# A recurrent attention and mixing kernel on one core: scores of half-blocks that are always zero left out, and DMAs dealt out to other queues

## The chip, the core and the metric

The kernel runs on one core of a Trainium2 chip. TensorE multiplies matrices, VectorE and ScalarE do elementwise work, GpSimd does a little of it and issues DMAs, and SyncE only issues DMAs. The metric is the device time of one execution in microseconds (us), and less is better. A run of "before" gave 459.9 us in the median of three (458.04 to 461.52).

## The reference

Two stages follow each other. The first is a gated linear recurrence over 768 time steps for 4 batches and 8 heads of 48 channels; the second is a channel-mixing layer with a width of 384 and an inner width of 1024. Everything is float32.

```python
mag = sqrt(a_re**2 + a_im**2); scale = minimum(mag, 0.999) / (mag + 1e-6)
for t in range(768):                         # per batch and head, S is 48x48
    S = (a_re + i*a_im)[t] * scale[t] * S + k[t] (x) v[t]     # complex S, k and v real
    y[t] = q[t] @ real(S)
x  = y with the heads side by side           # (4, 768, 384)
xk = mu_k * x + (1 - mu_k) * x_previous_step ;  xr likewise with mu_r
v  = relu(xk @ w_k)**2 @ w_v
out = sigmoid(xr @ w_r) * v
```

## The kernel before

**Tiling.** The 4 x 768 steps are cut into eight units of 384 steps (`U`); two units make a batch, and the second of the two continues the state of the first. A unit has three chunks of 128 steps (`NC`). For a unit u, `gate(u)` loads the gates, keys and queries (tile `g`) and the values (tile `v`), turns the gates into running logs and phases on ScalarE and VectorE, and multiplies keys and queries by them in place, so that the recurrence becomes a masked attention inside a chunk and a state carried between chunks. `attend(u)` does that attention: `stack(h)` copies one head's scaled real and imaginary parts of keys and queries by small DMAs from `g` into a `kq` buffer of 112 rows (48, a gap of 16 that is zero, 48); `scores(h)` multiplies keys by queries for the three chunks of one head into a PSUM bank (tile `sc`, line 885), and VectorE multiplies the result by a triangular mask of zeros and ones into `pt` (line 889); `advance(c)` transposes the keys (tile `tr`) and adds keys times values (`up`) to the state; `values(p)` computes the output of two heads, one in each half of the array's columns (tile `y`, line 908 from `pt`, line 915 from the state). Small DMAs move the result `ys` into the transposed activations `xt` (line 930). `mix(u)` forms the mixed inputs, and on TensorE the r gate (three products, tile `z`), the first layer (eight products, also `z`) and the second (eight, tile `o`). From the second unit on, each float32 operand is split into two parts of a faster float32 form, so that a product is nine matmuls instead of three.

**Masked half-blocks.** The scores of a chunk are a block of 128 keys by 128 queries. A key later than the query counts for nothing: the mask has zeros there. So the quarter of 64 late keys by 64 early queries is computed and multiplied by zero.

**Order of the work.** Nothing is ordered by hand. Every step is handed to a planner (class `Plan`) with its engine, an estimated cost, what it reads and writes and which buffers it uses. The planner works out due times backwards from a position in TensorE's work (the table `AT` gives each unit's attention and mixing a stretch) and then plays the execution through; a free engine takes the ready operation that is due first. The order in which operations started in the play is the order in which they are put into the engines' queues, and an engine goes through its queue strictly in order. In that play SyncE's and GpSimd's DMAs have a time line each (`dma[e]`), as if both could transfer at full rate beside each other.

**Queues.** SyncE's queue issues the first unit's `g` loads, the stack moves (line 816), the `xt` moves (line 930) and the stores (line 537). GpSimd's issues all bulk loads else: `g` of the later units (651), `v` (658), the weights (`raw`, 363) and a second load of the weights for a range test (`again`, 627), whose steps are spread over the whole run. GpSimd also clears the gap rows of the six `kq` buffers at the start (351). While the first mixing is not ready, TensorE gets filler products (`warm`, line 966).

Of the kernel before, what the change touches and what calls it, by code (L numbers as in the profile page):

```python
# [11 lines left out]
F32 = mybir.dt.float32  # L12
# [9 lines left out]
C = H * D  # L22
# [7 lines left out]
NP = H // 2  # L30
HR = 64
YS = 3
# [11 lines left out]
AT = ((0.38, 0.74), (1.0, 1.45), (1.28, 1.33), (2.34, 3.3), (2.2, 2.89), (3.4, 4.43), (3.07, 3.65), (4.24, 5.39),  # L44
      (4.34, 4.39), (4.94, 6.44), (5.25, 5.8), (7.11, 7.17), (6.14, 7.38), (7.41, 9.17), (7.2, 7.7), (9.54, 10.42))
PAIRS = 0, 1, 2, 3
# [5 lines left out]
RB = 4  # L52
SIG = 2.5
PTS = 3
# [4 lines left out]
FILL = ("r0", 0, 0), ("z", 0, 0)  # L59
NATIVE = 1  # L60
# [9 lines left out]
class Plan:  # L70
# [11 lines left out]
    QUEUE = dict(SP=0.63, GP=1.1)  # L82
    START, ARRIVE = 1.15, 0.9
    TURN = {("once", "half"): 0.09, ("full", "half"): 0.09,
# [71 lines left out]
    def run(self):  # L156
# [13 lines left out]
        dma = dict.fromkeys(self.QUEUE, 0.0)  # L170
        work = {}
        free, held, got = {}, dict.fromkeys(self.bufs, 0), dict.fromkeys(self.bufs, 0)
        taken, waiting, events, ends, order = set(), {}, [self.BEGIN], [], []
# [7 lines left out]
        def can(i):  # L181

            if ready[i] > t or (ops[i]["table"] and ops[i]["table"] != tables[-1]):
                return False
# [9 lines left out]
        while len(order) < len(ops):  # L194
# [7 lines left out]
            while found:  # L202
                found = False
                for e, queue in list(waiting.items()):
# [29 lines left out]
                    if e in self.QUEUE:  # L234
                        free[e] = t + self.QUEUE[e]
                        dma[e] = max(dma[e], t + self.START) + cost
                        end = dma[e] + self.ARRIVE
# [33 lines left out]
def tile_kernel(ctx, tc, gat, vt, w_all, mu, slow_g, slow_v, out):  # L271
# [51 lines left out]
    def op_dma(n, f, **kw):  # L323

        plan[0].op("SP", n / 360, f, **kw)

    def op_dma_gp(n, f, **kw):

        plan[0].op("GP", n / 300, f, **kw)
# [5 lines left out]
    mask = keep.tile([P, P], F32, name="mask")  # L335
    nc.gpsimd.memset(mask, 1.0)
    nc.gpsimd.affine_select(out=mask, in_=mask, pattern=[[1, P]], compare_op=ALU.is_ge,
                            fill=0.0, base=0, channel_multiplier=-1)
# [11 lines left out]
    for t in kqs:  # L350
        nc.gpsimd.memset(t[32:HR], 0.0)
# [17 lines left out]
    def open_mix(stack):  # L369
# [3 lines left out]

    bufs = dict(ps=5, o=1, xr=1, xk=1, zr=1, x=3, r=RB, hhi=HB, hlo=HB,
                look=1, g=GP, v=5, sq=1, m=1, ph=1, kq=KQ, kt=2, pt=PTS, xt=1, ys=YS)

# [3 lines left out]
    def sigmoid(u):  # L380
        op_act(NT * U, lambda: act(zr[u], zr[u], AF.Sigmoid), table=(u + SIG, "sigmoid"), reads=[("zr", u, mt) for mt in range(NT)],
               writes=[("r", u)], uses=[zr_slot[u]])

    def mix(u, native=False):
# [3 lines left out]
        part_slot = [slot("xr")] * 2 if native else [slot("xk"), slot("xr")]  # L388
        zr_slot[u] = slot("zr")

        def begin(ct):
# [7 lines left out]
            for which in (1, 0):  # L399
                if native:  # L400
                    def whole(which=which):
                        if not hi:
                            x = mp["x"].tile([P, NT, 2, U], F32, tag="xr", name="x")
                            hi.update({0: x[:, :, 0], 1: x[:, :, 1]})
# [48 lines left out]
        def gate_r(mt):  # L453
            sp = slot("ps")
# [5 lines left out]
            def out_():  # L460
                if u not in zr:
                    zr[u] = mp["h"].tile([P, NT, U], F32, tag="zr", name="zr", bufs=1)
                nc.scalar.copy(out=zr[u][:, mt], in_=tiles["z", mt])
            op_pe(cost, mul, kind=kind, reads=parts(1) + [(w_key, W_R + ct) for ct in range(NT)], writes=[("z", u, mt)],
                  uses=[sp, part_slot[1]])
            op_act(U, out_, psum=True, reads=[("z", u, mt)], writes=[("zr", u, mt)], uses=[sp, zr_slot[u]])
        gates_r = [lambda mt=mt: gate_r(mt) for mt in range(NT)]
        if u != NATIVE:
            steps += gates_r
# [56 lines left out]
        if u == NATIVE:  # L526
            steps += gates_r

        def end(mt):
            sr = slot("r")  # L530

# [4 lines left out]
            def store():  # L536
                nc.sync.dma_start(out=out[b, mt * P:(mt + 1) * P, half * U:(half + 1) * U], in_=tiles["y", mt])
# [587 lines left out]
```

## Time and profile before

| what | value |
|---|---|
| runs (us) | 459.9, 458.04, 461.52 |
| profiled execution | 460.59 us, its span 458.6 us |
| granted TensorE clock, mean | 0.945 |
| TensorE busy | 399.6 us, 87% of the span |
| ScalarE, VectorE busy | 341.6 us (74%), 329.3 us (72%) |
| GpSimd busy | 52.2 us (11%) |
| DMA | 67.51 MB |

The span runs from the first to the last instruction of the profiled execution. Times in rows are us from the start of the span unless marked ns. PEld is the loading of weights, which overlaps products. A float32 matmul of this kernel leaves two records. A row names the line of the kernel, the engine, the operation, and the tile written and those read.

### The profile page before, as it was taken

The numbers are of one execution on the slowest core, as the hardware profiler recorded it, in microseconds if no ns is written. First come the engines' busy times: TensorE is split into PE (matmuls) and PEld (weight loads), VectorE is DVE, ScalarE is ACT, GpSimd is POOL, SyncE is SP. The second block draws the span as 40 slices with busy tenths as digits, with TensorE's granted clock in tenths as the row PEclk, the third lists the DMA queues.
The fourth block names the chain that finished last, engine by engine and source line by source line (L and its number), as shares of the span: only waits on it lengthen the run. The fifth ranks groups of instructions, "written<-read, shape, count | busy, mean of one in ns | idle before, by whom it ended". The sixth has DMA issues, their size and how long they took to land.

```text
span 458.6 us, 8780 instructions
## 1 busy us (share of the span) xinstructions
PE 399.6 (87%) x3263; PEld 362.6 (79%) x3263; DVE 329.3 (72%) x536; ACT 341.6 (74%) x591; POOL 52.2 (11%) x116
## 2 busy tenths in 40 slices
PE   2005998999977999999999999999899998999994
PEld 2004995567666999999898989999799997899993
DVE  1599868669849988878886888777897866185222
ACT  5689755987768799989978799789879943563530
POOL 8510020000201120030003000011000000100000
PEclk8555999999978999999999999999999999999998
DMA  8996380602885827383647345268541455300001
GB/s 284 411 410 178 95 290 2 134 22 66 262 189 154 286 55 179 121 281 118 148 127 245 120 112 146 66 216 226 134 135 47 118 135 144 112 4 22 32 1 59
DMA packets 25074, 67.51 MB, mean 147 GB/s; under 512 B 5696, under 2 KB 11840, under 8 KB 25024
## 3 DMA queue, kind: packets, MB, share of 16 engines
q1 hardware_dynamic: 17520, 30.69, 25.6%
q0 software_dynamic: 7504, 36.18, 23.3%
q8 instruction: 28, 0.46, 0.4%
q14 instruction: 22, 0.18, 0.1%
HBM read 38.54 MB, written 4.72 MB: 94 GB/s over the span
## 4 chain that ended last, share of the span: by engine, by line
PE 56%; DMA 16%; ACT 10%; DVE 10%; issue 4%; SPq 2%; POOL 2%; DVEq 0%; ACTq 0%; POOLq 0%
PE z L444 18%; PE o L515 13%; PE sc L885 8%; DMA raw<-in_w_all 4%; DMA xt<-ys 4%; PE y L908 3%; PE o L512 3%; PE up L867 3%; DMA again<-in_w_all 3%; PE y L915 3%; PE z L439 3%; DMA kq<-g 3%; PE tr L847 2%; ACT r L295 2%; SPq L816 1%
## 5 line engine op out<-in xcount | busy, mean ns | idle before, releaser
L444 PE MATMUL z<-x,w 128*128 128x384 f32 x693 | 132.1, 340 | 0.0
L444 PEld LDWEIGHTS z<-x,w 128*128 128x128 f32 x693 | 120.6, 188 | 0.7 <-issue 0.7
L515 PE MATMUL o<-hhi,w 128*128 128x384 f32 x336 | 87.7, 342 | 0.0
L885 PE MATMUL sc<-kq 112*128 112x128 f32 x384 | 57.7, 297 | 5.8 <-DMA kq<-g 4.8
L515 PEld LDWEIGHTS o<-hhi,w 128*128 128x128 f32 x336 | 59.9, 188 | 0.6 <-issue 0.5
L885 PEld LDWEIGHTS sc<-kq 112*128 112x128 f32 x384 | 50.6, 204 | 11.0 <-issue 7.6
L515 PE MATMUL o<-hlo,w 128*128 128x384 f32 x168 | 57.1, 340 | 2.3 <-DVE hlo L496 2.2
L847 PE MATMUL tr<-ident,g 128*128 128x128 f32 x120 | 20.3, 298 | 36.2 <-DVE g L784 36.2
L847 PEld LDWEIGHTS tr<-ident,g 128*128 128x128 f32 x120 | 15.9, 153 | 39.3 <-DVE g L784 37.3
L484 ACT ACTIVATE r<-z 128x384 f32<-128x384 f32 x64 | 30.8, 483 | 20.6 <-PE z L444 20.0
L784 DVE TENSOR_TENSOR g<-g,r 128x768 f32<-128x768 f32 x48 | 43.1, 954 | 3.1 <-ACT r L295 2.9
L889 DVE TENSOR_TENSOR pt<-sc,mask 128x384 f32<-128x384 f32 x64 | 34.6, 552 | 5.4 <-PE sc L885 4.7
L515 PEld LDWEIGHTS o<-hlo,w 128*128 128x128 f32 x168 | 31.5, 188 | 3.9 <-DVE hlo L496 3.9
L423 ACT CAST x<-xm 128x384 fp32r<-128x384 f32 x42 | 21.1, 512 | 17.5 <-DVE xm L415 15.1
L488 ACT ACTIVATE h<-r 128x384 f32<-128x384 f32 x64 | 33.0, 520 | 0.8
L496 DVE TENSOR_TENSOR hlo<-h,hhi 128x384 fp32r<-128x384 f32 x56 | 30.9, 554 | 2.4 <-ACT hhi L311 1.0
L295 ACT ACTIVATE sq<-m 128x1152 f32<-128x1152 f32 (+2 forms) x27 | 28.0, 1054 | 6.1 <-DVE m L732 3.7
L908 PE MATMUL y<-pt,v 128*64 128x128 f32 (+1 forms) x384 | 29.3, 280 | 3.0 <-DVE pt L889 3.0
L311 DVE CAST hhi<-h 128x384 fp32r<-128x384 f32 x33 | 11.8, 358 | 25.9 <-PE o L515 13.4
L908 PEld LDWEIGHTS y<-pt,v 128*64 128x64 f32 (+1 forms) x384 | 20.8, 129 | 11.5 <-issue 5.8
L289 ACT ACT_TABLE_LOAD x22 | 28.2, 1283 | 1.2 <-PEq L1114 0.8
L627 POOL DMA_DIRECT2D again<-in_w_all x19 | 10.2, 539 | 161.9 <-ACT again L634 114.4
(85 smaller groups left out, 687.9 us busy)
## 6 DMA issues: line engine op xcount, KB each, us to landing
kq<-g SPq DMA_DIRECT2D x96, 144.0 KB, 3.4
g<-in_gat POOLq DMA_DIRECT2D x18, 768.0 KB, 6.4
again<-in_w_all POOLq DMA_DIRECT2D x19, 384.0 KB, 3.7
raw<-in_w_all POOLq DMA_DIRECT2D x9, 768.0 KB, 10.3
v<-in_vt POOLq DMA_DIRECT2D x24, 192.0 KB, 6.2
out_t<-y SPq DMA_DIRECT2D x24, 192.0 KB, 3.2
xt<-ys SPq DMA_DIRECT2D x48, 72.0 KB, 3.2
kq<-g SPq DMA_DIRECT2D x32, 96.0 KB, 3.1
```

The costliest lines, as they stand in the source:

```text
L289: nc.scalar.add_instruction(mybir.InstLoadActFuncSet(name=nc.get_next_instruction_name(), act_func_set_id=loaded[0], engine=mybir.EngineTy ...
L295: nc.scalar.activation(out=out, in_=in_, func=func, **kw)
L444: nc.tensor.matmul(z, lhsT=wt[s[0]][:, part, s[1]], rhs=r[which][:, ct], start=n == 0, stop=n == 3 * NT - 1)
L484: nc.scalar.activation(out=t["r", j], in_=t["f", j], func=AF.Relu)
L488: nc.scalar.activation(out=t["h", j], in_=t["r", j], func=AF.Square)
L496: nc.vector.tensor_tensor(out=t["lo", j], in0=t["h", j], in1=t["hi", j].bitcast(F32), op=ALU.subtract)
L515: nc.tensor.matmul(tiles["o", mt], lhsT=wt[W_V + 2 * j][:, part, ts(mt, P)], rhs=r, start=j == 0 and n == 0, stop=j == NJ - 1 and n == 2)
L784: nc.vector.tensor_tensor(out=g[:, ct, 2 * i:2 * i + 2], in0=g[:, ct, 2:4], in1=t["r"][:, ct, 1 - i:2 - i].to_broadcast([P, 2, U]), op=ALU ...
L847: nc.tensor.transpose(out=t["tr", c, part][:, ct * P:(ct + 1) * P], in_=G[u][:, ct, 2 * part, c * P:(c + 1) * P], identity=ident)
L885: nc.tensor.matmul(sc[:, c], lhsT=kq[h][:, 0, ts(c, P)], rhs=kq[h][:, 1, ts(c, P)], start=True, stop=True)
L889: nc.vector.tensor_mul(pts[h], t["sc", h], mask.unsqueeze(1).to_broadcast([P, NC, P]))
L908: nc.tensor.matmul(t["y", p][rows, ts(c, P)], lhsT=V[u][c][:, cols], rhs=pts[hs[j]][:, c], start=c == 0, stop=False)
```

## The change

It has these parts.

1. `scores(k, c)` handles two pairs of heads and one chunk instead of one head and three chunks. Each head is done as two products: the 64 early keys by all 128 queries, and the 64 late keys by the 64 late queries; late keys by early queries are left out. The two heads of a pair use opposite halves of the array's columns. The result of a pair lies in three times 64 columns, and one VectorE instruction per operation takes it apart into two heads by an overlapping access pattern and applies the mask, now all-ones or zero integers, by a bitwise AND over 512 columns. For the second head of a pair the rows come out with the two half-blocks of keys exchanged, so `v` carries a second copy of every second head, rolled by 64 rows: its rows grow from 384 to 576 columns.
2. The four pairs run in the order 0, 3, 1, 2; the scores of two pairs are followed by the values of both.
3. Queues: `g` of the units from 2 on, `v` from unit 1 on and the second weight load go to SyncE's queue; stack moves and `xt` moves may go to either queue, as the planner finds one free. The planner now keeps one DMA time line for both queues, starts a bulk DMA only when that line is not too far behind, and has other costs for issuing (GpSimd 0.65 instead of 1.1 us).
4. The r gate's three products come last in every unit's mixing (before: only in one unit), its sigmoid is taken in three pieces of 384 columns instead of one of 1152, and the final product is written in place. The filler ends with the first product of the first layer.
5. The `kq` gaps are cleared by VectorE; the mask is made by eight small selects on GpSimd. Two more `kq` buffers for the first unit lie in the space of the first unit's mixed input (`x0`).
6. Buffers: `r` 6 for 4 (it now also holds the r gate), `pt` 4 for 3 (of 512 columns instead of 384), `v` 4 for 5, `kt` 1 for 2, `ys` 2 for 3. The table `AT` has other numbers.

The core of the diff:

```diff
-PAIRS = 0, 1, 2, 3
+PAIRS = 0, 3, 1, 2
-FILL = ("r0", 0, 0), ("z", 0, 0)
+FILL = ("r0", 0, 0), ("f", 0, 0)
-    QUEUE = dict(SP=0.63, GP=1.1)
+    QUEUE = dict(SP=0.63, GP=0.65)
+    BULK = 0.4
...
+            if o["engine"] in self.QUEUE and o["cost"] > self.BULK and dma > t + self.START:
+                return False
...
+    def op_move(n, f, **kw):
+        plan[0].op("SP", n / 380, lambda e: f(nc.sync if e == "SP" else nc.gpsimd), other={"GP": n / 380}, **kw)
...
-        nc.gpsimd.memset(t[32:HR], 0.0)
+        nc.vector.memset(t[32:HR], 0.0)
...
-        op_act(NT * U, lambda: act(zr[u], zr[u], AF.Sigmoid), ...
+        for mt in range(NT):
+            op_act(U, lambda mt=mt: act(zr[u, mt], zr[u, mt], AF.Sigmoid), ...
...
-                nc.gpsimd.dma_start(out=raw.bitcast(I32), in_=w_all[:, i * C:(i + 1) * C].bitcast(I32))
+                nc.sync.dma_start(out=raw.bitcast(I32), in_=w_all[:, i * C:(i + 1) * C].bitcast(I32))
...
-                    (nc.gpsimd if u else nc.sync).dma_start(out=G[u][:, ct, part], in_=gat[b, half, ct, :, part])
+                    (nc.gpsimd if u == 1 else nc.sync).dma_start(out=G[u][:, ct, part], in_=gat[b, half, ct, :, part])
...
-                    v = ap.tile([P, C], F32, tag="v", name="v", bufs=5)
-                    nc.gpsimd.dma_start(out=v, in_=vt[b, half, c])
+                    v = ap.tile([P, C + C // 2], F32, tag="v", name="v", bufs=VB)
+                    (nc.sync if u else nc.gpsimd).dma_start(out=v, in_=vt[b, half, c])
...
-            def scores(h):
+            def scores(k, c):
...
-                    for c in range(NC):
-                        nc.tensor.matmul(sc[:, c], lhsT=kq[h][:, 0, ts(c, P)], rhs=kq[h][:, 1, ts(c, P)], start=True, stop=True)
+                    for i, p in enumerate(ps2):
+                        for late in range(2):
+                            for j in range(2):
+                                rows = slice((j ^ late) * Q, (j ^ late) * Q + Q)
+                                q = kq[2 * p + j][:, 1, c * P + late * Q:(c + 1) * P].rearrange("p (b t) -> p b t", t=Q)
+                                cols = slice((1 + late) * Q if j else 0, 3 * Q if j else (2 - late) * Q)
+                                nc.tensor.matmul(sc[rows, i, cols], lhsT=kq[2 * p + j][:, 0, c * P + late * Q:][:, :Q],
+                                                 rhs=q if j else q[:, ::-1], start=True, stop=True)
...
-                    nc.vector.tensor_mul(pts[h], t["sc", h], mask.unsqueeze(1).to_broadcast([P, NC, P]))
+                    both = bass.AP(tensor=sc.tensor, offset=sc.offset, ap=[sc.ap[0], sc.ap[1], [Q, 2], [1, P]])
+                    nc.vector.tensor_tensor(out=pts[k, c].bitcast(I32), in0=both,
+                                            in1=masks.unsqueeze(1).to_broadcast([P, 2, 2, P]), op=ALU.bitwise_and)
...
+            steps += stacks(0) + all_scores(0) + stacks(1)[:2] + adv + [begin] + stacks(1)[2:]
+            a, *rest = all_scores(1)
+            steps += [a] + both(0) + rest + both(1)
```

171 lines of the change are left out of this document (93 added, 78 removed).

## The prediction

> **What bounds the kernel now.** I read the page first (busy shares and the chain that ended last), then the busy times by stretches of 20 us, then the chain in order of time, and last the timelines of the stretches where TensorE is not full. The first fence has two lines of the page's busy shares and chain, and rows of the stretches (us of the stretch; then busy time and instructions of PE, PEld, DVE, ACT, POOL; granted clock; DMA share; GB/s).
>
> ```profile
> PE 399.6 (87%) x3263; PEld 362.6 (79%) x3263; DVE 329.3 (72%) x536; ACT 341.6 (74%) x591; POOL 52.2 (11%) x116
> ...
> PE 56%; DMA 16%; ACT 10%; DVE 10%; issue 4%; SPq 2%; POOL 2%; DVEq 0%; ACTq 0%; POOLq 0%
> ```
>
> ```profile
> 0.00:20.00 20.00, 2.93 (x12) 2.64 (x12) 4.68 (x9) 10.61 (x21) 14.48 (x40) 0.72 0.90 338
> 20.00:40.00 20.00, 0.47 (x1) 0.18 (x1) 19.95 (x29) 17.96 (x28) 3.42 (x5) 0.50 0.92 354
> ...
> 60.00:80.00 20.00, 18.55 (x121) 14.51 (x122) 14.11 (x21) 10.87 (x15) 2.21 (x4) 1.00 0.37 132
> ...
> 120.00:140.00 20.00, 16.06 (x186) 13.13 (x184) 12.18 (x21) 13.71 (x22) 1.61 (x3) 0.83 0.85 213
> 140.00:160.00 20.00, 17.65 (x137) 16.09 (x136) 18.22 (x31) 15.10 (x27) 3.73 (x7) 0.91 0.76 230
> ...
> sum 460.00, PE 399.60 PEld 362.59 DVE 329.29 ACT 341.62 POOL 52.16; mean PE 17.37 PEld 15.76 DVE 14.32 ACT 14.85 POOL 2.27
> ```
>
> The 87% hides three stages. For 40 us TensorE has nothing to do (2.93 + 0.47 us busy, nearly all of it warming). From there to the end it is nearly full: 399.6 - 3.4 = 396.2 us busy. Between 120 and 160 us it idles for 6.3 (40 - 16.06 - 17.65), and the granted clock fell to 0.83 and 0.91 there. So time comes off in two ways: less TensorE work in the full stage, or an earlier start of it. The chain in order of time (start, duration, what) shows who sets the start and the hole after 120 us; the timeline rows (start, duration, instruction, in brackets the idle time before and its releaser) belong to the same places.
>
> ```profile
> 2.27 4.11 POOL kq L351 x6
> ...
> 13.48 9.79 DMA raw<-in_w_all
> ...
> 63.20 5.54 DMA xt<-ys
> ...
> 121.96 8.43 DMA kq<-g
> ```
>
> ```profile
> 8.18 0.56 DVE L690 SCALAR_TENSOR_TENSOR ph<-ph,g 128x384 f32<-128x384 f32 x1 [7.22 <-ACT ph L295]
> ...
> 15.73 0.56 ACT L578 ACTIVATE raw<-raw 128x384 int32<-128x384 uint8 x1 [5.02 <-DMA raw<-in_w_all]
> ...
> 40.20 1.33 PE L847 MATMUL tr<-ident,g 128*128 128x128 f32 x5 [4.07 <-DVE g L784]
> ...
> 61.12 8.30 PE L966 MATMUL warm<-mask,ident 128*128 128x128 f32 x72
> ...
> 128.78 3.31 PE L885 MATMUL sc<-kq 112*128 112x128 f32 x12 [3.46 <-DMA kq<-g]
> ...
> 450.80 1.62 DVE L534 TENSOR_TENSOR y<-o,zr 128x384 f32<-128x384 f32 x3 [1.19 <-PE o L515]
> ...
> 451.48 0.34 PE L515 MATMUL o<-hlo,w 128*128 128x384 f32 x1
> ```
>
> The reader is to see that at the start ScalarE stands 5.02 us before a weight conversion whose load has not landed, while the first gate's own steps wait behind it in its order. The loads began only after GpSimd had spent 4.11 us clearing the kq buffers. The 8.30 us of warm products at 61 us are filler, not work. At 122 us two stack moves take 8.43 us, and TensorE waits 3.46 us for them. The last product ends at 451.8: from 40 us on, about 412 us hold 396 of work, so only 16 are idle, those 6.3 among them.
>
> **The change part by part. Scores.** Here are TensorE rows of one steady unit.
>
> ```profile
> 185.10 2.17 PE L867 MATMUL up<-v,kt 128*64 128x48 f32 x64
> ...
> 191.11 1.60 PE L885 MATMUL sc<-kq 112*128 112x128 f32 x12
> 192.47 1.81 PE L444 MATMUL z<-x,w 128*128 128x384 f32 x9
> 194.21 0.87 PE L908 MATMUL y<-pt,v 128*64 128x128 f32 x12
> 194.91 0.83 PE L915 MATMUL y<-kq,state 112*48 112x128 f32 x12
> 195.66 1.60 PE L885 MATMUL sc<-kq 112*128 112x128 f32 x12
> ```
>
> An fp32 product leaves two records, so the 12 of sc are two heads of three chunks. From its start to that of z are 1.36 us, 5.44 us per unit of eight heads. The new operation takes two pairs of heads and one chunk. Per pair it issues two 64-row products of 128 queries, one in each half of the array, and two of 64 queries. I price the first by y: 12 records, three couples of halves, 194.91 - 194.21 = 0.70 us, so 0.233 a couple. The couple of 64 queries has no row. From below it is half of that, 0.117; from above it is the up row, where 16 couples of 48 columns take 2.17 us, 0.136 each, so there instructions and weight loads, not columns, set the pace. I take 0.136, since it is the row with short products. An operation is then 2 x (0.233 + 0.136) = 0.74 us, six are 4.43, and a unit saves 1.01; with 0.117 it is 4.20 and 1.24. Over eight units that is 8.1 to 9.9 us.
>
> Changing between halves and the full array costs as well: y's second group takes 0.75 up to sc where its first takes 0.70. Scores and values are now of one kind, so some changes go, but scores between two z products gain two of them, and z takes 1.74 from 192.47 to the start of y. I put this at -0.25 us a unit, between -0.5 and +0.5. **Scores: -10 us, from -5 to -14.** What could hide that saving is a rival below. The Trainium skill, TensorEngine Tiling (Array Packing), section Instruction Overhead, gives about 60 cycles as the floor of one product, so 64 columns would still pay by columns; by that rule the saving is the 9.9 above, by the up row it is 8.1, and no run here shows which yet.
>
> **VectorE, ScalarE.** These groups (busy us, mean ns) price the rest.
>
> ```profile
> L784 DVE TENSOR_TENSOR g<-g,r 128x768 f32<-128x768 f32 x48 | 43.1, 954 | 3.1 <-ACT r L295 2.9
> L889 DVE TENSOR_TENSOR pt<-sc,mask 128x384 f32<-128x384 f32 x64 | 34.6, 552 | 5.4 <-PE sc L885 4.7
> L588 DVE SCALAR_TENSOR_TENSOR raw<-raw 128x768 int32<-128x768 int32 x9 | 8.4, 948 | 0.0
> L488 ACT ACTIVATE h<-r 128x384 f32<-128x384 f32 x64 | 33.0, 520 | 0.8
> L295 ACT ACTIVATE zr<-zr 128x1152 f32<-128x1152 f32 x8 | 9.3, 1167 | 0.1
> L351 POOL MEMSET kq<- 32x768 f32 x6 | 4.1, 730 | 0.1
> L337 POOL TENSOR_SCALAR_AFFINE_SELECT mask<-mask 128x128 f32<-128x128 f32 x1 | 0.3, 292 | 0.0
> L627 POOL DMA_DIRECT2D again<-in_w_all x19 | 10.2, 539 | 161.9 <-ACT again L634 114.4
> ```
>
> The mask becomes a 512-wide AND on integers, 48 times. Integer bit work runs as float does (948 against 954 ns at 768), and between 552 at 384 and 954 at 768 lies 686 at 512: 48 x 0.686 = 32.9 us against 64 x 0.552 = 35.3. The split sigmoid is 24 x 0.52 = 12.5 us for 9.3, ScalarE +3.2. Both engines are below three quarters busy and TensorE's queue covers them: zero, at worst +3 if ScalarE became the bound.
>
> **Start.** The kq clearing leaves GpSimd: -4.11. Eight quarter-size selects come, each at most the 0.292 of the whole one, 0.8 to 2.3 us together, and the old mask's select goes. The bulk stream thus begins 2 to 3.5 us earlier. VectorE takes over the clearing, about eight pieces of 0.73 = 5.8 us, under its 7.22 us of idle before its first step; if it were twice as slow there, the first gate would slip 4 us. The planner now counts both queues' transfers as one stream, so a conversion should not be put ahead of its load, and the 5.02 us wait can shrink too. Against this v rows grow by half, for two units 0.6 MB early, 1.7 us at 354 GB/s. VectorE is full between 20 and 40 us, so not all arrives: **-3, from +4 to -9**. The stack moves and the 5.54 us of xt moves behind the first attention may then use two queues.
>
> **The hole at 120 to 160 us.** DMAs by group (KB each, median us to landing):
>
> ```profile
> kq<-g SPq DMA_DIRECT2D x96, 144.0 KB, 3.4
> g<-in_gat POOLq DMA_DIRECT2D x18, 768.0 KB, 6.4
> ...
> v<-in_vt POOLq DMA_DIRECT2D x24, 192.0 KB, 6.2
> ```
>
> GpSimd's own timeline at that place:
>
> ```profile
> 115.29 1.58 POOL L651 DMA_DIRECT2D g<-in_gat  x3 [45.00 <-ACT r L772]
> 121.82 1.61 POOL L658 DMA_DIRECT2D v<-in_vt  x3 [4.95 <-PE y L908]
> ```
>
> The stack moves usually land in 3.4 us; here 8.43, beside these three g and three v loads. In the change bulk is held back while the modelled stream is behind, and small moves spread over two issuers (0.539 us each on GpSimd, idle most of the time, so the issue is covered). Wholly gone it is 3.46 us of waiting, and of the slow clock (33.7 us busy at about 0.87) up to 4.4. **-4, from 0 to -8.**
>
> **The end.** The receptance gate's products now stand behind the second products of each unit, and the end was shown above. Today only the VectorE product and the store follow the last TensorE work. With the gate last, a copy and a sigmoid piece come between, two times 0.52: **+1**. Fewer kt, ys and v buffers (1 for 2, 2 for 3, 4 for 5) and more r and pt buffers have no row; I take zero, from -2 to +3, since the planner orders by them.
>
> Sum: -10 - 3 - 4 + 1 = -16 on the profiled execution's 460.6, so 444.6; the median of the runs is 0.7 lower, so **444 us**.
>
> **The rivals.** *TensorE stops being the bound.* The chain is 56% TensorE only, and 36% of it is DMA, ScalarE and VectorE. If those loops set the middle, the score time turns into idle TensorE, and only the other terms stay: 460 - 6 = 454. For it speaks that share; against it that of 412 us only 16 are idle today, so those loops do keep pace with TensorE. Chance 0.18. *Bulk in front of small moves, the slower side.* The loads of g and v and the second look at the weights now sit in SyncE's queue with stack moves, xt moves and stores. On GpSimd the look loads stood 114.4 us behind ScalarE at no cost; on SyncE, whatever waits there holds all moves behind it, and TensorE's scores and z wait for those. Besides, one 768 KB load takes 2.2 us at 354 GB/s, three of them 6.7, which a move behind them adds to its 3.4. It decides when it reaches TensorE in each of the six later units: with 2.7 us each the gain of 16 is gone, with the 6.7 the time is 444 + 40 = 484, with half of them 464. Against it: the orders come from one modelled clock, so the drift should be small, and TensorE's z products, 1.74 us each, cover short waits. Chance 0.1, at 465. The Trainium skill, DMA: Bandwidth & Descriptors, section Queues, rings and completion order, says that engines take turns between queues and go through one ring in order; by that rule bulk of the other queue shares with a move while bulk of its own queue goes first. The 8.43 us beside foreign bulk shows the sharing; no run here shows the other half yet. *The retuned order closes more.* If the other 10 us of idle TensorE outside 120 to 160 us and the start's -9 come as well, about 432; chance 0.12. *It does little*: moves and order cancel the scores, 459; chance 0.05. My forecast keeps 0.55.
>
> **How the numbers follow.** About 1% is what a measurement here can tell from no change: below 455.3 is faster, above 464.5 slower. Forecast and the deep rival (0.67) are faster, and of the first rival (454, at the edge) 0.11 of 0.18: 0.78. Same: 0.07 + 0.05 = 0.12. Slower 0.10. The range leaves out the slower rival and half of the deepest: 431 to 458. The forecast's own terms alone would make it 436 to 453.
>
> **What would show it.** Right: the sc products of a unit near 4.4 us for 5.4; first transposes at about 37 us; no wait of several us for kq moves near 120 us; the end with a sigmoid after the last products. Wrong: SyncE's queue waiting long on an `again`, g or v load with moves behind it; TensorE with more idle time after 160 us than now; VectorE's clearing ending after 8 us; or score rows that cost as much as before because the halves do not run side by side.

## The result: slower by 4%, where 3% faster was forecast

The changed kernel took 483.3 us in the median of four runs (477.4 to 487.5), the kernel before, run beside it, 459.6. The ratio is 1.043, with a 95% interval from 1.033 to 1.053; it leaves out two disturbed runs of the four, and the other two, 477.42 and 481.24 us, have a mean of 479.3 us, which is the time of after in all comparisons below. The second of these is the profiled execution of after; its span is 479.5 us.

The page of after, busy shares and the chain that ended last:

```profile
PE 402.3 (84%) x3625; PEld 361.6 (75%) x3625; DVE 331.3 (69%) x523; ACT 346.1 (72%) x611; POOL 78.8 (16%) x179
...
PE 36%; DMA 20%; issue 14%; ACT 13%; DVE 12%; POOL 3%; SPq 1%; POOLq 0%; DVEq 0%; ACTq 0%
```

TensorE is on 36% of the chain, where it was on 56%. Its idle time grew from 59.0 us (458.6 - 399.6) to 77.2 (479.5 - 402.3), and although a quarter of the score work is gone, it is busy for 2.7 us more. The stretches of 20 us show where (columns as in the prediction):

```profile
20.00:40.00 20.00, 5.41 (x27) 4.62 (x29) 19.63 (x27) 19.06 (x27) 5.81 (x11) 1.00 1.01 343
40.00:60.00 20.00, 14.09 (x226) 13.17 (x225) 10.76 (x16) 10.78 (x17) 2.93 (x6) 0.83 0.63 164
...
120.00:140.00 20.00, 13.44 (x147) 11.08 (x146) 13.48 (x23) 13.20 (x25) 3.79 (x8) 0.83 0.75 163
...
340.00:360.00 20.00, 17.47 (x231) 15.83 (x232) 12.45 (x23) 17.41 (x33) 2.98 (x6) 0.74 0.42 115
```

TensorE has work earlier than before (5.41 us of it between 20 and 40 us, a part of it filler, where there were 0.47). From there on holes come in most parts of the run, not only at 120 us, and with many of them the granted clock falls. Before, between 60 us and the last products it was below 1.00 in two stretches only, those from 120 and from 140 us. What TensorE waited for, in after (engine, line, releaser: us in total, times, longest):

```profile
PE tr L865 <- DVE g L797: 31.2, 2, 25.5
PE sc L914 <- DMA kq<-g: 20.5, 18, 5.9
PE up L885 <- ACT kt L871: 8.4, 6, 3.4
```

The same view of before has this line for the scores:

```profile
PE sc L885 <- DMA kq<-g: 4.8, 2, 3.5
```

So the scores wait 18 times for stack moves, 20.5 us in all, where they waited twice, for 4.8. The chain of after in order of time has a stack move at the start of the attention of one unit after another:

```profile
34.95 10.12 DMA kq<-g
...
173.70 7.64 DMA kq<-g
...
228.42 8.96 DMA kq<-g
...
330.26 6.90 DMA again<-in_w_all
...
389.49 5.35 DMA kq<-g
```

The load at 330.26 is a piece of the second weight load, handed in while eight stack moves were still under way. VectorE stood 4.9 us for it and ScalarE then 4.7, each in its own order, ScalarE's copy `kt` came late, and TensorE's state products waited 3.39 us for that. So crowded moves reach TensorE by other engines as well.

One of the places with stack moves in the timeline of after (start, duration, what; in brackets the idle time before and its releaser):

```profile
170.96 6.44 SPq L834 DMA_DIRECT2D kq<-g  x7
...
172.35 2.10 POOL L834 DMA_DIRECT2D kq<-g  x4 [0.36 <-issue]
...
181.47 1.31 PE L914 MATMUL sc<-kq 112*64 112x128 f32 x24 [1.81 <-DMA kq<-g]
...
185.66 1.24 PE L914 MATMUL sc<-kq 112*64 112x128 f32 x16
```

Both queues issue stack moves at once. No load is under way beside them; the last one landed at 170.62. The scores stop in the middle for the last of the moves, and the next operation of 16 records takes 1.24 us: the granted clock was half from 183.0 to 186.4 us. Issue and landing of the moves at this place, read out of the trace (us, queue, landing minus issue):

```
170.96 -> 174.05  SyncE   3.09      172.96 -> 178.07  GpSimd  5.12
171.49 -> 174.97  GpSimd  3.49      173.06 -> 179.01  SyncE   5.94
171.83 -> 175.99  SyncE   4.16      173.45 -> 179.76  GpSimd  6.31  (96 KB)
172.35 -> 177.02  GpSimd  4.66      173.70 -> 181.34  SyncE   7.64
172.43 -> 177.43  SyncE   5.00 (96 KB)  173.94 -> 181.36  GpSimd  7.42
```

They are issued 0.33 us apart in the mean and land 0.81 us apart; the lag grows from 3.1 to 7.6 us. In before, with one queue and no load under way either, six moves of such a place were issued 0.64 us apart (217.94 to 221.15) and landed at 220.98, 222.19, 222.55 (96 KB), 223.53, 224.48 and 224.72 (96 KB). From the first landing to the last that is 168 thousand bytes per us in after and 171 in before, so about 0.9 us for a move of 144 KB in both. **The second issuer doubled the rate at which moves are handed in and left the rate at which they land.** The planner's `op_move` divides a move's 147 thousand bytes by 380, so it counts 0.39 us where 0.9 to 1.0 are used (1.0 us would be 147 thousand bytes per us, the price tried below).

At the first attention loads come on top. Two weight loads of GpSimd's queue (issued at 31.31 and 31.88, landed at 40.35 and 42.59) are under way there, and no stack move lands between 34.97 and 43.59. So the 10.12 us of the chain at 34.95 are not the pace of the moves alone, and neither is the longest of the 18 waits, 5.9 us, which follows.

### The profile page after: what moved, and what is told of

The parts are those of the page before. It is cut to its first block, busy times and chain, and to the rows that moved or that the text cites. A ratio compares the mean times of both kernels' runs of the same rounds, so it can differ in the third digit from the quotient of the medians.

```text
span 479.5 us, 9560 instructions
## 1 busy us (share of the span) xinstructions
PE 402.3 (84%) x3625; PEld 361.6 (75%) x3625; DVE 331.3 (69%) x523; ACT 346.1 (72%) x611; POOL 78.8 (16%) x179
## 4 chain that ended last, share of the span: by engine, by line
PE 36%; DMA 20%; issue 14%; ACT 13%; DVE 12%; POOL 3%; SPq 1%; POOLq 0%; DVEq 0%; ACTq 0%
PE z L461 11%; DMA kq<-g 11%; PE o L528 9%; PE sc L914 4%; DMA again<-in_w_all 4%; PE up L885 3%; DMA raw<-in_w_all 2%; DVE g L797 2%; DMA xt<-ys 2%; PE y L949 2%; PE o L525 2%; DVE ph L764 2%; PE y L955 2%; PE tr L865 1%; ACT r L303 1%
## 5 line engine op out<-in xcount | busy, mean ns | idle before, releaser
L528 PE MATMUL o<-hhi,w 128*128 128x384 f32 x336 | 89.0, 346 | 0.0
L834 POOL DMA_DIRECT2D kq<-g x77 | 39.0, 509 | 227.8 <-PE y L955 150.8
L914 PE MATMUL sc<-kq 112*64 112x64 f32 (+1 forms) x744 | 52.2, 283 | 25.2 <-DMA kq<-g 20.5
L914 PEld LDWEIGHTS sc<-kq 112*64 112x64 f32 x744 | 44.7, 159 | 35.0 <-issue 25.0
L865 PE MATMUL tr<-ident,g 128*128 128x128 f32 x120 | 22.0, 315 | 31.2 <-DVE g L797 31.2
L923 DVE TENSOR_TENSOR pt<-sc,masks 128x512 int32<-128x512 int32 x48 | 31.6, 684 | 23.8 <-PE sc L914 23.7
L970 POOL DMA_DIRECT2D xt<-ys x40 | 21.8, 546 | 91.5 <-ACT ys L964 84.6
L871 ACT COPY kt<-tr 128x384 f32<-128x384 f32 x40 | 18.1, 473 | 21.7 <-PE tr L865 21.5
L885 PE MATMUL up<-v,kt 128*48 128x48 f32 (+1 forms) x640 | 25.5, 234 | 9.1 <-ACT kt L871 8.4
L885 PEld LDWEIGHTS up<-v,kt 128*48 128x48 f32 (+1 forms) x640 | 23.4, 145 | 12.2 <-ACT kt L871 11.2
## 6 DMA issues: line engine op xcount, KB each, us to landing
kq<-g POOLq DMA_DIRECT2D x51, 144.0 KB, 5.5
kq<-g SPq DMA_DIRECT2D x43, 144.0 KB, 5.5
```

The lines of the kernel that those rows point to most:

```text
L528: nc.tensor.matmul(tiles["o", mt], lhsT=wt[W_V + 2 * j][:, part, ts(mt, P)], rhs=r, start=j == 0 and n == 0, stop=j == NJ - 1 and n == 2)
L834: queue.dma_start(out=kq[h][i * HR + o:i * HR + o + n], in_=G[u][s, ct, 2 * i:2 * i + 2])
L865: nc.tensor.transpose(out=t["tr", c, part][:, ct * P:(ct + 1) * P], in_=G[u][:, ct, 2 * part, c * P:(c + 1) * P], identity=ident)
L885: nc.tensor.matmul(t["up", c][rows, h * D:(h + 1) * D], lhsT=both[:, cols], rhs=V[u][c][:, h * D:(h + 1) * D], start=True, stop=True)
L914: nc.tensor.matmul(sc[rows, i, cols], lhsT=kq[2 * p + j][:, 0, c * P + late * Q:][:, :Q], rhs=q if j else q[:, ::-1], start=True, stop=True)
L923: nc.vector.tensor_tensor(out=pts[k, c].bitcast(I32), in0=both, in1=masks.unsqueeze(1).to_broadcast([P, 2, 2, P]), op=ALU.bitwise_and)
```

## The experiments

The kernel's planner plays the order through before anything runs, and the length of that play can be set beside the chip: 426.0 us in before and 424.8 in after. The chip took 34 and 55 us longer. For after I matched ScalarE's operations in the trace with the play, one by one. Until 31 us of the play they are on time (0.8 us late); they are 9 us late at 42 us of the play, 21 at 120, 28 at 187, 38 at 262, 47 at 322, 53 at 375, and every single step of 2.5 us or more falls on a stretch in which a unit's heads are stacked and their scores computed.

Five causes were named in the expectations. **A**: the price of a move in the planner. **B**: bulk loads in SyncE's queue, ahead of the moves (the slower rival of the prediction). **C**: the new scores, which need four heads at once. **D**: an unlucky table `AT`. A table fits one planner (the table of after, with another price of moves, gives a play of 457.3 us instead of 424.8), so every kernel below whose planner differs has a table chosen for its own shortest play, except e8, and the play's length stands beside its time. **E**: that the gain of a dearer move comes from the planner's rule that holds back whatever is costly, and not from its price. Since each has its own order, differences of 2 or 3 us between two of them say little.

### The price of a move (e1_price)

```diff
-        plan[0].op("SP", n / 380, lambda e: ..., other={"GP": n / 380}, **kw)
+        plan[0].op("SP", n / 147, lambda e: ..., other={"GP": n / 147}, **kw)
```

> The changed kernel, with the planner told that a small move runs at 147 GB/s instead of 380 (144 KB in 1.0 us, the pace at which the moves land in both profiles), and the table AT searched anew for that planner (its plan 428.3 us; that of the changed kernel was 424.8, that of the kernel before 426.0, and they took 55 and 33 us more on the chip). Theory A, the planner starts scores too early because it underprices the moves: the plan is kept about as well as before, 428 + 30 to 35 = 458 to 463 us, and TensorE's waits for kq moves fall from 20.5 us to under 8. Theory B, bulk loads in SyncE's queue hold the moves up: the queues are as in the changed kernel, so about 475 to 483. Theory C, scores that need four heads at once wait at the start of each unit whatever the price: 470 to 480.

Measured: 434.35 us (433.6 to 436.4), ratio to before 0.942 [0.934, 0.950], with a play of 428.3, which the chip misses by 6 us. That is better than theory A said (458 to 463): it had kept the 30 to 35 us by which before misses its play, and most of those went too. The computation is that of after; the order and the filler differ, and so do the queues. In after 51 of the stack moves of 144 KB stand in GpSimd's queue, and here none (queue, count, KB each, median us to landing):

```profile
kq<-g SPq DMA_DIRECT2D x94, 144.0 KB, 3.1
```

One number in the planner, and the table and order that follow from it, take 45 us off (479.3 to 434.35). How much of that is the price and how much the choice of queue, e9 and e11 below take apart. The page of this kernel:

```profile
PE 386.7 (89%) x3687; PEld 351.8 (81%) x3687; DVE 332.9 (77%) x525; ACT 342.2 (79%) x609; POOL 50.4 (12%) x116
...
PE 68%; DVE 13%; DMA 7%; ACT 6%; issue 3%; POOL 1%; SPq 0%; DVEq 0%; ACTq 0%; POOLq 0%
```

What TensorE waited for in it:

```profile
PE up L885 <- ACT kt L871: 2.7, 5, 0.9
...
PE sc L914 <- DMA kq<-g: 0.4, 1, 0.4
```

The wait for stack moves is gone, 0.4 us for 20.5, and ScalarE, matched with its play as above, is never more than 4.4 us late. The two timelines of TensorE at the first attention show how. After:

```profile
39.85 1.07 PE L885 MATMUL up<-v,kt 128*64 128x48 f32 x31
...
40.82 0.51 PE L914 MATMUL sc<-kq 112*64 112x128 f32 x7
47.24 2.28 PE L914 MATMUL sc<-kq 112*64 112x128 f32 x24 [5.91 <-DMA kq<-g]
```

With the right price:

```profile
41.74 2.84 PE L1008 MATMUL warm<-ident 128*128 128x128 f32 x24
44.51 1.13 PE L885 MATMUL up<-v,kt 128*64 128x48 f32 x32
...
46.05 0.77 PE L914 MATMUL sc<-kq 112*64 112x128 f32 x10
47.23 1.89 PE L914 MATMUL sc<-kq 112*64 112x128 f32 x38 [0.42 <-DMA kq<-g]
```

In after the order put scores in at 40.8, when the planner believed the heads to be there. TensorE goes through its queue in order, so it stood for 5.91 us, with transposes and state products behind the waiting scores, and then ran at half clock (24 records in 2.28 us; here 38 in 1.89). With the right price state products, transposes and filler stand in front, and the scores begin 5 us later and run through. The last move that they need, behind weight loads in both, is there at the same time, 47.2 us; what differs is what TensorE does until then.

Of the 47.0 us between the two spans (479.5 - 432.5), 31.4 are idle time of TensorE and 15.6 busy time, and 15.9 of busy time is sc alone (52.2 and 36.3 us by the groups): products broken up by waits and run at half clock. Read out of the clock records from 46 us to the last product, after was at half clock for about 37 us, before for about 10. Of the 37, 27 follow waits of the scores, for moves above all, and 10.2, from 340.0 us, belong to the wait for `kt` told above. In e1 no stretch of 20 us between 20 and 420 us is below 1.00.

### One part at a time (e2, e3, e4)

e2_scores_only has the new scores, buffers and start, with the DMA model and queues of before; e3_queues_only has the new queues and model, with the old scores; e4_syncE_moves is after with all moves on SyncE's queue, still at 0.39 us.

```diff
 e2  -    QUEUE = dict(SP=0.63, GP=0.65)
     +    QUEUE = dict(SP=0.63, GP=1.1)
     -            if o["engine"] in self.QUEUE and o["cost"] > self.BULK and dma > t + self.START:
     -                return False
     ...  two DMA time lines, moves on SyncE at n / 360, bulk on GpSimd at n / 300
 e3  -            def scores(k, c):
     +            def scores(h):
     ...  values, mask and order of before
 e4  -        plan[0].op("SP", n / 380, lambda e: f(nc.sync if e == "SP" else nc.gpsimd), other={"GP": n / 380}, **kw)
     +        plan[0].op("SP", n / 380, lambda: f(nc.sync), **kw)
```

> The changed kernel with the queues and the planner's DMA model of the kernel before (all bulk by GpSimd's queue, all small moves by SyncE's, two DMA time lines, issue costs 0.63 and 1.1 us); the new scores, buffers and order of the gate stay. AT searched anew for it (plan 427.7 us). Theory A (moves look twice as fast in the plan with two issuers as with one): the plan is missed by about what it was before, 427.7 + 33 to 40 = 461 to 468. Theory B (bulk in front of the moves): also 461. Theory C (four heads at once): 475 to 483, as the scores are as in the changed kernel.

> The changed kernel with the scores of the kernel before (one head, three chunks, full array, mask by multiplication, three pt buffers, the order of steps of before); queues, planner, other buffers and gate order stay as changed. AT searched anew (plan 428.2 us). Theory A: moves by two queues are underpriced here too, 428 + 45 to 55 = 473 to 483. Theory B: the same, 473 to 483. Theory C: the fault lies in the scores' four heads, so the plan is missed by 33 as before: 461.

> The changed kernel with all small moves by SyncE's queue, behind the bulk loads that it issues; the planner's price of a move stays at 0.39 us, but the issue of 0.63 us each paces them in the plan. AT searched anew (plan 426.7 us). Theory A: the plan is off by 0.4 us a move instead of 0.6, so 426.7 + 40 to 45 = 467 to 472. Theory B: all moves now sit behind bulk, so no better than the changed kernel, 480 or more. Theory C: 470 to 480.

Measured: e2 469.2 us (play 427.7), ratio 1.018 [1.009, 1.027]; e3 470.5 (play 428.2), 1.020 [1.012, 1.029]; e4 452.7 (play 426.7), 0.980 [0.973, 0.988]. So e2 and e3 miss their plays by about 42 us each, e4 by 26. e2 lies just above what A expected (461 to 468), e3 just below (473 to 483), and e4 is faster than any of the three theories had it. The scores' wait in e2, in e3 and in e4:

```profile
PE sc L911 <- DMA kq<-g: 11.5, 14, 2.6
```

```profile
PE sc L899 <- DMA kq<-g: 10.5, 5, 3.4
```

```profile
PE sc L914 <- DMA kq<-g: 4.5, 8, 1.4
```

Each part alone loses 2%, and the waits for moves are only some 11 of the 42 us that e2 and e3 miss; the rest is not taken apart. The new scores need four heads before their first product instead of one, so a late move is felt 14 times instead of twice (C plays a part), and the two queues hand in moves faster than they land (e3). Taking the second issuer away is worth 27 us (479.3 to 452.7): on one queue, issuing at 0.63 us each paces the moves in the play as well, and hides a part of the wrong price. For B, e4 is a plain miss: all its moves stand behind bulk in SyncE's queue, which should have been no better than after.

### Other tables, the price in other places (e5 to e8)

e5_other_table is after with only another `AT`, whose play is as short (424.7 us). e6_before_price is the kernel before with its moves priced by 147. e7_old_scores_price is e1 with the old scores. e8_price_same_table is after with the price alone, and the table that it had, with which the play gets 457.3 us long.

```diff
 e5  -AT = ((0.51, 1.23), (0.86, 1.42), (2.31, 2.4), ...
     +AT = ((1.93, 3.11), (0.01, 0.66), (0.44, 1.59), ...
 e6  -                    op_dma(n * 3.07, f, ...
     +                    op_dma(n * 3.07 * 360 / 147, f, ...
 e7  the edit of e1 and that of e3
 e8  the edit of e1 without its new AT
```

> The changed kernel with nothing but another table AT, found by the same search for the changed kernel's own planner (moves at 380 GB/s); its plan is 424.7 us, that of the change 424.8. Theory A (the price of the moves): the plan is missed as before, 424.7 + 45 to 55 = 470 to 480 us. Theory D (the change's table was an unlucky one, and e1 gained by its new table): near e1, 430 to 445.

> The kernel before with the stack moves and xt moves priced at 147 GB/s in its planner and its table searched anew (plan 427.7 us); queues, scores and all else as before. Theory A: the before kernel's plan was 33 us off partly for the same reason; with honest moves it is off by 10 to 20 (its two DMA time lines still hide that bulk and moves share the engines), 438 to 448. Theory D: within 455 to 464.

> The queues and planner of the change with moves at 147 GB/s, but the scores of the kernel before (as in e3), table searched anew (plan 428.8 us, e1's was 428.3). If leaving the quarter of the scores out is worth its TensorE time only where TensorE is the bound, and the plans say that with honest moves the two are alike: 435 to 440. If the scores' 21 us of TensorE time (57.7 us before, 36.3 in e1) shows in full: 450 to 456.

> The changed kernel with the moves priced at 147 GB/s and its own table AT kept, which does not fit that planner (plan 457.3 us). Theory A: the plan is kept, missed by 5 to 15 us, so 462 to 472, faster than the changed kernel's 483 though its plan is 32 us longer. Theory D: the price alone does not help, 483 or more.

Measured:

```
                      median   ratio to before           play   missed by
e5_other_table         480.6   1.045 [1.039, 1.052]      424.7   56
e6_before_price        454.0   0.987 [0.984, 0.991]      427.7   26
e7_old_scores_price    441.9   0.960 [0.953, 0.966]      428.8   13
e8_price_same_table    467.3   1.020 [1.012, 1.028]      457.3   10
```

e5 is as slow as after, and its scores wait as long:

```profile
PE sc L914 <- DMA kq<-g: 25.3, 16, 5.6
```

So another table of the same length brings nothing. e8 keeps the table and changes the price alone:

```profile
PE sc L914 <- DMA kq<-g: 2.2, 3, 1.0
```

Its play is 32 us longer than that of after, its table was made for another model, and yet the chip is 12 us faster with it (479.3 to 467.3), because the order now fits what the DMA does. The two together refute D and speak for A. e6 disappoints. I expected the price to be worth more in the kernel before; it gave 1.3%, and 26 us are still missed. What is left there is not settled; its play still has two DMA time lines that each run at full rate, which was not tried apart. Matched with its play, its ScalarE is 24 us late at the end, and the largest step, 5.2 us, is the first weight conversion, which stands 5.7 us before its load.

e7 against e1 gives what the new scores are worth once moves are priced rightly: 441.9 - 434.35 = 7.6 us, with plays of 428.8 and 428.3. It lies between the two forecasts (435 to 440 and 450 to 456), and it is one table against one table, so 2 or 3 us of it may be the order.

### Is it the price alone? (e9, e10, e11)

A move priced at 1.0 us falls under the rule that holds bulk back (costs over `BULK`, 0.4), so e9_no_hold takes moves out of that rule. e10_bulk_gpsimd is e1 with `g`, `v` and the second weight load on GpSimd's queue, as before. e11_price_syncE is e1 with all moves on SyncE's queue.

```diff
 e9   -            if o["engine"] in self.QUEUE and o["cost"] > self.BULK and dma > t + self.START:
      +            if o["engine"] in self.QUEUE and o["cost"] > self.BULK and not o["other"] and dma > t + self.START:
 e10  -                nc.sync.dma_start(out=raw.bitcast(I32), in_=w_all[:, i * C:(i + 1) * C].bitcast(I32))
      +                nc.gpsimd.dma_start(out=raw.bitcast(I32), in_=w_all[:, i * C:(i + 1) * C].bitcast(I32))
      ...  the same for g and v
 e11  -        plan[0].op("SP", n / 147, lambda e: ..., other={"GP": n / 147}, **kw)
      +        plan[0].op("SP", n / 147, lambda: f(nc.sync), **kw)
```

> e1 with the small moves exempted from the planner's rule that holds a DMA back while the modelled stream is behind (at 147 GB/s a 144 KB move costs 1.0 us in the plan and so falls under that rule, at 380 GB/s it did not). Moves stay priced at 147 GB/s; table searched anew (plan 436.3 us). Theory A, the price alone: the plan is kept, missed by 5 to 15 us, 441 to 451. Theory E, it is the holding back that helped e1: missed by 30 or more, 466 and up.

> e1 with all bulk loads back on GpSimd's queue as in the kernel before (g from unit 1 on, v, the second weight load); moves by either queue at 147 GB/s; table searched anew (plan 431.7 us). Theory B (bulk in SyncE's queue costs): the plan is missed by less than e1's 6 us, and the time is below 438. If it does not matter which queue the bulk stands in: missed by 5 to 15, 437 to 447.

> e1 with all small moves on SyncE's queue, at 147 GB/s; table searched anew (plan 430.5 us). If a second queue for moves brings no transfer speed, only issue time: missed by 5 to 12 as e1, 435 to 443. If the second queue is worth what the change meant it to be: 450 and up.

Measured: e9 439.7 us (play 436.3), ratio 0.958 [0.954, 0.962]; e10 452.0 (play 431.7), 0.983 [0.978, 0.988]; e11 437.4 (play 430.5), 0.954 [0.949, 0.958].

In e9 the moves crowd both queues again and land as late as in after. Its DMA issues (queue, count, KB each, median us to landing), then the scores' wait:

```profile
kq<-g POOLq DMA_DIRECT2D x54, 144.0 KB, 5.8
...
kq<-g SPq DMA_DIRECT2D x40, 144.0 KB, 4.8
```

```profile
PE sc L914 <- DMA kq<-g: 0.7, 1, 0.7
```

The same two issue lines of after are these:

```profile
kq<-g POOLq DMA_DIRECT2D x51, 144.0 KB, 5.5
...
kq<-g SPq DMA_DIRECT2D x43, 144.0 KB, 5.5
```

The landing times are alike, both queues are used alike, and TensorE waits 0.7 us instead of 20.5. So E is refuted, the queue that the moves stand in is not what counted, and a late landing alone does not make TensorE wait: what the order believed of it did. The play of e9 is 8 us longer than that of e1, so the later landings are not free, but they are planned for. That is the cleanest separation of these runs.

e11, with one queue for all moves, is no slower than e9 with two, so once the price is right the second issuer brings the stack moves nothing. In e1 it carries only `xt` moves and small stack moves, and e11 is 3 us behind e1, no more than two orders may differ by. e10 lies outside both its forecasts (below 438, and 437 to 447). It speaks against B, as e4 does, and for the opposite: with bulk on the other queue the kernel is some 18 us slower, 3 of them in its play already. The DMA issues of e10, and then of e1:

```profile
v<-in_vt POOLq DMA_DIRECT2D x24, 288.0 KB, 5.3
...
xt<-ys SPq DMA_DIRECT2D x26, 72.0 KB, 4.0
```

```profile
v<-in_vt SPq DMA_DIRECT2D x21, 288.0 KB, 3.6
...
xt<-ys SPq DMA_DIRECT2D x24, 72.0 KB, 2.6
```

With bulk in SyncE's queue the `v` loads land sooner (3.6 for 5.3 us), and so do SyncE's `xt` moves (2.6 for 4.0). Why e10 misses its play by 20 us is only partly shown: its lateness grows in many steps of 1 to 3 us, and TensorE's state products wait 8.0 us for ScalarE's `kt`, where they wait 2.7 in e1.

### The pace by itself (e12)

e12_pace is e1 with 15 moves of 144 KB from one `kq` buffer to another after all other work: five by SyncE, five in turn by both, five by GpSimd. It adds work that the reference doesn't have, so its time (454.8 us, one run) is of no interest.

```diff
+    for j in range(1, 6):
+        nc.sync.dma_start(out=kqs[j][HR:HR + D], in_=kqs[0][:D])
+    for j in range(5):
+        (nc.gpsimd if j % 2 else nc.sync).dma_start(out=kqs[j][:D], in_=kqs[5][HR:HR + D])
+    for j in range(1, 6):
+        nc.gpsimd.dma_start(out=kqs[j][HR:HR + D], in_=kqs[4][:D])
```

> e1 with fifteen more moves of 144 KB between kq buffers after the last check of the run, each set behind the one before: five by SyncE's queue, five alternating between SyncE's and GpSimd's, five by GpSimd's. Their data are not used and nothing is left out; the time grows by some 20 us and is not of interest. Theory A: they land about 1.0 us apart on one queue and on two alike. If two queues move faster: 0.5 to 0.6 us apart when alternating.

The issues of the second and third group in its timeline:

```profile
435.46 1.00 POOL L1048 DMA_DIRECT2D kq<-kq  x2 [51.03 <-DMA kq<-kq]
436.49 2.75 SPq L1048 DMA_DIRECT2D kq<-kq  x3
442.34 2.62 POOL L1050 DMA_DIRECT2D kq<-kq  x5 [5.88 <-DMA kq<-kq]
```

Landings, read out of the trace (us):

```
both queues   438.28  439.31  440.37  441.11  441.79   0.88 apart, issued 0.63 apart
GpSimd alone  444.92  446.15  447.20  448.14  448.72   0.95 apart, issued 0.53 apart
```

Stores of the last unit fall between SyncE's five, so those give no clean pace. GpSimd alone issues every 0.53 us and lands every 0.95; two issuers land every 0.88. In the second group GpSimd's two came first and SyncE's three behind them, so it was handed in no faster than the third; what a doubled hand-in does is shown by the burst at 170.96 us in after. In all of them the pace is 0.9 to 1.0 us for 144 KB, and a second queue adds some 8% at most. The Trainium skill says as much in DMA: Bandwidth & Descriptors, section Issuing engines are not separate DMA queues: DMAs of all engines run on the same 16 DMA engines, and issuing from more of them only saves the time to issue. The trace agrees (0.95 and 0.88 us).

## Why the prediction was wrong

**The step that failed is the hole at 120 to 160 us.** It read the 8.43 us of two stack moves as the work of six bulk loads beside them, which fits the trace of before (of the moves issued from 118.2 us on none lands before 126.0, while the three `g` loads land at 119.9, 122.1 and 126.7). But it concluded that "small moves spread over two issuers (0.539 us each on GpSimd, idle most of the time, so the issue is covered)", and booked -4 us. Issuing was never the limit: with no bulk in the way moves landed about 0.9 us apart then too, from one queue. The page that I read gave 144.0 KB and 3.4 us to landing; I took the 3.4 us for a latency and didn't look at how far apart landings of a burst lie, nor set that beside the planner's price, which stands in the diff (`n / 380`). Instead of -4 the term was +15.7 for waits for moves (20.5 against 4.8 us), and on top of it about 27 us more at half clock than before (37 against 10), worth some 13 us by estimate, half of them. State products waiting for `kt` add 7.7 (8.4 against 0.7). The prediction had put fewer `kt` buffers at zero; e1 has as few and waits 2.7, so at most 2 of the 7.7 are theirs. With the scores' -9 and 5 us won at the start that makes 22, near the 20.9 between the spans (479.5 - 458.6). A sign that the prediction had named for being wrong is there too: from 160 us to the last product TensorE is idle for 21.0 us, before for 7.2.

**Scores: right.** Six operations were to cost 4.43 us a unit. Rows of e1's TensorE, with z behind them in a steady unit:

```profile
168.68 2.23 PE L914 MATMUL sc<-kq 112*64 112x128 f32 x48
170.84 1.83 PE L461 MATMUL z<-x,w 128*128 128x384 f32 x9
```

Three operations take 2.16 us, so a unit 4.32 for the 5.44 of before: between the bounds of 4.20 and 4.43, worth 9.0 us over eight units. The couple of 64 queries then has (4.32 / 6 - 2 x 0.233) / 2 = 0.127 us, between the two prices of 0.117 and 0.136. The 7.6 us from e7 to e1 are of the size of the -10, within its range of -5 to -14, where TensorE is not made to wait. The halves do run side by side; by form of e1's groups:

```profile
L914 PE MATMUL sc<-kq 112*64 112x128 f32 x372 | 34.1, 278 | 0.5 <-DMA kq<-g 0.4
...
L914 PE MATMUL sc<-kq 112*64 112x64 f32 x372 | 27.8, 221 | 0.0
```

Their busy times add to 61.9 us, and the whole group covers 36.3. A product of 64 queries takes 221 ns, one of 128 takes 278: halving the queries saves a fifth. The Trainium skill's floor of about 60 cycles a product (TensorEngine Tiling (Array Packing), section Instruction Overhead), by which 64 columns would still pay by columns, was one end of the bounds; the measured 0.127 lies half way to the other.

**VectorE and ScalarE: the prices were right.** The group of the mask in after, and the split sigmoid:

```profile
L923 DVE TENSOR_TENSOR pt<-sc,masks 128x512 int32<-128x512 int32 x48 | 31.6, 684 | 23.8 <-PE sc L914 23.7
...
L303 ACT ACTIVATE zr<-zr 128x384 f32<-128x384 f32 x24 | 12.5, 525 | 0.4
```

The AND takes 684 ns (predicted 686), the sigmoid 525 (520).

**Start: right, and given back at once.** TensorE's first transposes:

```profile
28.83 0.47 PE L865 MATMUL tr<-ident,g 128*128 128x128 f32 x1 [25.47 <-DVE g L797]
35.07 0.69 PE L865 MATMUL tr<-ident,g 128*128 128x128 f32 x2 [5.77 <-DVE g L797]
```

The second group begins at 35.07, for 40.20 before and the 37 that I expected, so 5 us were won. Then the chain's 10.12 us for stack moves, with the weight loads beside them, took them: the scores ran on at 47.24 only, where those of before began at 41.32. VectorE's clearing ended before 8 us (at 5.78), and GpSimd's eight selects took 2.21 us, inside the 0.8 to 2.3.

**End: wrong, and worth nothing.** I put a copy and a sigmoid piece behind the last product. In after's timeline they are done 5 us ahead of it:

```profile
466.77 0.53 ACT L303 ACTIVATE zr<-zr 128x384 f32<-128x384 f32 x1
...
471.90 1.60 DVE L543 TENSOR_TENSOR zr<-o,zr 128x384 f32<-128x384 f32 x3 [1.64 <-PE o L528]
...
472.51 0.34 PE L528 MATMUL o<-hlo,w 128*128 128x384 f32 x1
```

From the end of the last product to the end of the span are 6.7 us (479.5 - 472.85), before 6.8 (458.6 - 451.82): 0 for +1.

**The rivals.** The slower side had the chance of 0.10 and the wrong mechanism: bulk ahead of moves in SyncE's queue. SyncE's queue did not hold moves behind bulk in a way that counts, and e10 is slower without that bulk; that its times, 465 to 484, lie about the measured one is luck. I had looked for queues that wait and not for the belief of the planner, although the change edits that belief in four places (one time line, 0.65 for 1.1 us, 380 for 360, 400 for 300). "The retuned order closes more", 432 us, is near e1 (434.35): such a gain was there, behind one wrong number. TensorE did not stop being the bound for lack of work; it was made to wait by its own order.

## What to carry to other kernels

Where a planner writes the order of in-order queues, its price for an operation can matter more than how long the operation takes: here moves that land after 5.5 us cost 20 us of waiting when they are believed to be quick and 0.7 when they are not. Before adding a second issuer, look at how far apart the landings of a burst lie; if they are further apart than the issues already, a second queue adds little, and it takes away what had kept the planner's error small. And when a planned order is changed, set the play beside the trace operation by operation: the first one that is late names the price that is wrong.

## What the runs showed of the hardware

- Moves of 48 rows of 3 KB inside SBUF land 0.9 to 1.0 us apart, 155 to 171 thousand bytes per us, from one queue or two (e12 and the bursts of before and after), where bulk loads of the same kernel reach 343 GB/s (after, the stretch from 20 to 40 us). The prediction had put no rate on them, and the planner had priced them at the rate of the bulk.
- Short waits are dear on TensorE because the granted clock halves with them: in after the half clock came in stretches of 3.4 us and multiples of it (3.4, 6.8, 10.2), 37 us in all, at waits of the scores and, from 340 us, of the state products. The Trainium skill, TensorE: Matmul & The Clock Gate, Part 1, has the same 3.4 us as the length of the window; the trace agrees.
- Bulk in the same queue as small moves was better for both than bulk in the other queue (`xt` moves 2.6 against 4.0 us, `v` 3.6 against 5.3). The same skill page on DMA, section Queues, rings and completion order, has DMA engines take turns between queues; that fits, but no run here isolates it, nor whether loads from GpSimd's queue land later in any case.
